# A new table of issue orders for an attention and two-mixer kernel on one core

## The chip, the cores and the metric

One core of a Trainium2 chip runs the kernel. Five engines of that core work at once: TensorE (PE, with its weight loads shown as PEld), VectorE (DVE), ScalarE (ACT), GpSimd (POOL) and SyncE (SP, which only issues DMAs). Each takes its instructions strictly in the order in which they stand in its own queue, and waits at one whose inputs or buffers are not ready, with everything behind it. The metric is the device time of one launch in microseconds.

## The reference

Float32 throughout. Attention for 4 batches, 12 heads, 448 tokens and head size 64, with an RMS norm on q and k; its output, laid out as 4 x 448 x 768, goes through two mixers.

```
q_n, k_n = rmsnorm(q, g_q), rmsnorm(k, g_k)
attn = softmax(q_n @ k_n.T / sqrt(64)) ; x = attn @ v
u = x + (x.T @ U @ V).T                    # mixer a, rank 32 over the tokens
x = u + relu(u @ w_ch1) @ w_ch2            # 768 -> 3072 -> 768
u = x + (relu(x.T @ w_tok1) @ w_tok2).T    # mixer b, 448 -> 256 -> 448
x = u + relu(u @ w_ch1) @ w_ch2            # 768 -> 1536 -> 768
```

## The kernel before

Every float32 operand of a product is kept as two rounded parts (hi and lo), and a product is three matmuls: hi by hi, lo by hi, hi by lo. So between two products an ACT instruction writes the hi part and a DVE or POOL instruction the rest. The channel weights come in as 64-bit words: `to_f32` (lines 123 to 141) rounds them on ACT (L132, L137), DVE (L133, L134, L138: tile `w_bits`) and POOL (L141), and `split` (L151 on ACT, L152 on POOL) makes the two parts.

The order of the work: attention of batches 0 and 1 alone (to about 180 us). Then mixer a on batches 0 and 1 while the attention of batches 2 and 3 runs beside it (to about 600 us), mixer b on batches 0 and 1 (to about 980 us), and then mixers a and b on batches 2 and 3, taken as a pair (`pair_ffn`) by a scheme that saves matmuls at the price of more additions on DVE and POOL.

Names that the text uses:

- `load_pair` squares q and k (L380, tile `sq`), sums (L381, `ms`), forms the scale (L383 to L391, `nt`, `rs`) and scales (L399, `qn`, `kn`). `turn_pair` transposes them on PE (L420, `tt`), and ACT and DVE write the parts (L427, L428, L431, L432, tile `both`), which DMAs place as `qs` and `ks`.
- `softmax` multiplies (`sc`), takes the maximum on DVE (L461, `nm`), the exponential on ACT (L463, `p`), and scales on POOL (L470). `weigh` transposes the probabilities on PE, four 112 x 112 blocks to a bank (L489, `pt`), splits them (L500, L504) and multiplies by v (`pv`).
- In the mixers `first` makes `ps_g`, and `relu` its parts (L657 on ACT, L658 on DVE, tile `gs`); `second` makes `ps_x`, which DVE adds to `xT` (L688), and so frees the bank. In `pair_ffn` the products are `ps_p` (first layer) and `ps_x` (second layer). DVE adds from PSUM in L781 and L853, ACT copies from PSUM in L803; `parted` (L786 on ACT, L787 on DVE) makes parts of sums that lie in SBUF; L799 is a difference, on POOL or on DVE; and `join` (L864 to L880) adds up large pieces at the end of each pair, on POOL (L864, L867, L868, L878) and DVE (L870, L873, L876, L880).

Which buffers are used, which instructions exist and what they compute is fixed by the code. The order on each engine is set at the end: `set_order` decodes the string `ORDER`, a list of displacements for each engine, and ties each instruction to the one that is to stand before it. It acts on the five queues alike, with the DMA issues on SP among them. Nothing else depends on `ORDER`.

Of the kernel before, what the change touches and what calls it, by code (L numbers as in the profile page):

```python
# [1166 lines left out]
def set_order(tc):  # L1167
# [172 lines left out]
```

## Time and profile before

| | |
|---|---|
| median of 3 runs | 1509.82 us (1508.5 to 1512.07) |
| the profiled execution | 1512.63 us |
| its span, first to last instruction | 1510.9 us |
| PE busy | 1435.4 us (95%), 7396 matmuls |
| DVE busy | 1193.6 us (79%) |
| POOL busy | 906.7 us (60%) |
| ACT busy | 737.5 us (49%) |
| mean granted TensorE clock | 0.99 |

An instruction's own time on DVE and POOL includes what it waits after it was started, so a row that is long for its kind shows such a wait inside the instruction, and not as idle time. Idle time stands in square brackets behind a row, with what ended it.

### The profile page before, as it was taken

How to read it: one execution, taken by the hardware profiler on the slowest of the kernel's cores; microseconds unless marked ns; L12 is line 12 of the kernel's file. 1: busy time of each engine (PE TensorE's matmuls, PEld its weight loads, DVE VectorE, ACT ScalarE, POOL GpSimd, SP SyncE). 2: the span in 40 equal slices, each digit the busy share in tenths (PEclk: the TensorE clock that was granted, in tenths of full speed). 3: DMA queues.
4: the chain of work that ended last, by engine and by line, in shares of the span. 5: the costliest groups of instructions: out<-in, count | busy, mean ns of one | idle time of the engine just before them, and what ended most of it. 6: DMA issues, size and time to landing. Idle time of an engine off the chain costs nothing.

```text
span 1510.9 us, 21970 instructions
## 1 busy us (share of the span) xinstructions
PE 1435.4 (95%) x7396; PEld 1262.2 (84%) x7396; DVE 1193.6 (79%) x1805; ACT 737.5 (49%) x1508; POOL 906.7 (60%) x943
## 2 busy tenths in 40 slices
PE   5999888999999999999999999999999998999998
PEld 3766666889888889888899998889889987999987
DVE  7998878887887887766867865777888888668886
ACT  4887755666656666334544443344433331335431
POOL 5999846787776665445664643067768864206760
PEclk9999989999999999999999999999999999999999
DMA  6775655776857765765457765445353453334343
GB/s 171 186 183 130 156 174 160 244 237 192 254 165 240 236 188 191 242 208 185 159 197 248 260 203 180 158 154 170 122 169 124 147 182 115 97 108 164 116 125 103
DMA packets 144384, 266.05 MB, mean 176 GB/s; under 512 B 12832, under 2 KB 104448, under 8 KB 144160
## 3 DMA queue, kind: packets, MB, share of 16 engines
q1 hardware_dynamic: 143952, 264.65, 56.5%
q8 instruction: 59, 0.97, 0.3%
q14 instruction: 53, 0.43, 0.1%
q10 hardware_dynamic: 320, 0.00, 0.0%
HBM read 149.72 MB, written 79.10 MB: 151 GB/s over the span
## 4 chain that ended last, share of the span: by engine, by line
PE 69%; DVE 13%; POOL 5%; DMA 5%; issue 3%; ACT 3%; SPq 1%; ACTq 0%; POOLq 0%; DVEq 0%
PE ps_x L81 26%; PE ps_g L81 16%; PE ps_p L81 9%; PE pv L81 4%; PE sc L81 4%; PE pt L489 3%; PE ps_u L81 2%; DVE gs L787 2%; PE ps_t L81 2%; DMA ks<-both 2%; DVE xT L853 1%; POOL p L470 1%; PE pt_x L572 1%; DVE pu L799 1%; DVE w_bits L133 1%
## 5 line engine op out<-in xcount | busy, mean ns | idle before, releaser
L81 PE MATMUL ps_x<-gs,w 128*128 128x448 f32 x1440 | 331.5, 371 | 9.2 <-DVE xT L688 8.7
L81 PE MATMUL ps_g<-u,w 128*128 128x448 f32 x1440 | 329.5, 372 | 3.8 <-DVE gs L658 2.6
L81 PEld LDWEIGHTS ps_x<-gs,w 128*128 128x128 f32 x1440 | 266.4, 189 | 36.3 <-DVE xT L688 13.3
L81 PEld LDWEIGHTS ps_g<-u,w 128*128 128x128 f32 x1440 | 268.8, 189 | 28.5 <-DVE gs L658 3.4
L81 PE MATMUL ps_x<-gs,w_b 128*128 128x448 f32 x1026 | 236.1, 372 | 14.4 <-DVE xT L853 7.2
L81 PEld LDWEIGHTS ps_x<-gs,w_b 128*128 128x128 f32 x1026 | 192.7, 190 | 36.9 <-DVE gs L787 6.9
L141 POOL TENSOR_TENSOR w_bits<-w_bits,w_round 128x768 uint32<-128x768 uint32 (+3 forms) x80 | 142.0, 1775 | 116.4 <-DVE w_bits L138 48.8
L152 POOL TENSOR_TENSOR w<-w_bits,w 128x768 fp32r<-128x768 f32 (+3 forms) x82 | 148.1, 1811 | 91.1 <-ACT w L151 71.2
L152 POOL TENSOR_TENSOR w_b<-w_f,w_b 128x384 fp32r<-128x384 f32 x104 | 120.9, 1183 | 97.1 <-ACT w_b L151 94.9
L688 DVE TENSOR_TENSOR xT<-ps_x,xT 128x448 f32<-128x448 f32 x216 | 131.4, 619 | 51.0 <-PE ps_x L81 49.1
L470 POOL TENSOR_SCALAR p<-p,sm 112x448 f32<-112x448 f32 x192 | 130.1, 687 | 35.9 <-DVE sm L467 30.4
L463 ACT ACTIVATE p<-sc,nm 112x448 f32<-112x448 f32 x192 | 120.9, 634 | 48.3 <-DVE nm L461 44.9
L461 DVE TENSOR_REDUCE nm<-sc 112x1 f32<-112x448 f32 x192 | 114.0, 616 | 18.1 <-PE sc L81 17.6
L81 PE MATMUL sc<-ks,qs 128*112 128x448 f32 x384 | 120.2, 404 | 6.4 <-ACT p L463 4.5
L489 PE MATMUL pt<-ident,p 112*112 112x112 f32 x768 | 110.5, 261 | 4.7 <-POOL p L470 3.8
L500 ACT ACTIVATE ph<-pt 112x448 fp32r<-112x448 f32 (+1 forms) x168 | 87.7, 543 | 54.6 <-PE pt L489 46.0
L489 PEld LDWEIGHTS pt<-ident,p 112*112 112x112 f32 x768 | 85.9, 133 | 29.6 <-issue 7.3
L787 DVE TENSOR_TENSOR gs<-pu,gs 128x448 fp32r<-128x448 f32 x98 | 97.1, 1009 | 9.3 <-ACT gs L786 9.2
L302 POOL TENSOR_TENSOR w_f<-w_f 128x384 f32<-128x384 f32 x26 | 28.9, 1112 | 124.8 <-DMA w_f<-c_a 83.6
L81 PE MATMUL ps_p<-t,w_b 128*128 128x448 f32 x432 | 97.0, 367 | 1.4 <-ACT pu L803 1.0
L132 ACT ACTIVATE w_bits<-w_raw 128x768 f32<-128x768 f32 (+3 forms) x80 | 69.7, 873 | 52.3 <-POOL w L152 26.1
L504 DVE TENSOR_TENSOR pl<-pt,ph 112x448 fp32r<-112x448 f32 x144 | 86.1, 616 | 11.1 <-ACT ph L500 10.4
(141 smaller groups left out, 2681.6 us busy)
## 6 DMA issues: line engine op xcount, KB each, us to landing
w_raw<-in_moe_w_ch_dram SPq DMA_DIRECT2D x72, 768.0 KB, 5.1
w_b<-h_a SPq DMA_DIRECT2D x65, 384.0 KB, 4.4
h_a<-w SPq DMA_DIRECT2D x56, 384.0 KB, 4.4
ks<-both SPq DMA_DIRECT2D x92, 224.0 KB, 4.2
c_a<-w_bits SPq DMA_DIRECT2D x40, 384.0 KB, 3.7
w_f<-c_a SPq DMA_DIRECT2D x40, 384.0 KB, 4.5
h_b<-w SPq DMA_DIRECT2D x32, 384.0 KB, 3.4
w_b<-h_b SPq DMA_DIRECT2D x29, 384.0 KB, 4.3
```

Of the source, the lines that this page charges most:

```text
L81: nc.tensor.matmul(o, lhsT=l, rhs=r, start=start, stop=stop)
L132: nc.scalar.activation(f(w), f(high), AF.Abs)
L141: nc.gpsimd.tensor_tensor(w, w, r, op=ALU.add)
L152: nc.gpsimd.tensor_sub(lo, w, f(hi))
L461: nc.vector.tensor_reduce(nm, sc, axis=AX.X, op=ALU.max, negate=True)
L463: nc.scalar.activation(p, sc, AF.Exp, bias=nm, accum_out=sm[:, c % 2:c % 2 + 1])
L470: nc.gpsimd.tensor_scalar(x, x, sm[:, i:i + 1], 1.0, op0=ALU.mult, op1=ALU.mult)
L489: nc.tensor.transpose(pt[:, c * CP:(c + 1) * CP], pr[c][:, kc * CP:(kc + 1) * CP], ident[:CP, :CP],)
L500: nc.scalar.activation(ph, pt, AF.Copy)
L504: nc.vector.tensor_sub(pl, pt, f(ph))
L688: nc.vector.tensor_add(xT[:, dc], px, xT[:, dc])
L787: nc.vector.tensor_sub(s[:, 1], t, f(s[:, 0]))
```

## The change

Only the string `ORDER` is replaced: 121 lines of it by 131. The same instructions with the same operands and buffers stand on each engine in another order. Most of them move by a few places: counted over the whole program, an instruction on PE moves by 5.6 places on the mean (82 at most), on DVE, ACT and POOL by 2.1, on SP by 2.6.

```diff
 ORDER = (
-    'c-rk<33B8(uDwtyLR>{f-~V2pz<VG;Ntt%Js;6gubeNE<(kY1x2x7<n+LxckpDn)*{%q}`r8-;xZg2fkX4_v|buCIu{RiJ'
...
+    'c-rlKiIUv9j_ePWBE(&a^Z)<#h|B~@sZ{N5+h^{~yon;zc9leN0YGd7_t$>=G<~-Gs`_llYwKT}_y-Da4gIslSK4RkPg&_'
...
 )
```

First place: DVE in mixer b of batches 0 and 1, about 631 to 640 us into the run. `w_bits_8019` and `w_bits_8221` are two blocks of raw weights in work, `gs_7842` and `gs_7864` the lo parts behind two first-layer products. Before:

```order
L138 SCALAR_TENSOR_TENSOR w_bits_8019<-w_raw_8017,w_bits_8019 128x768
L133 TENSOR_SCALAR w_bits_8221<-w_bits_8221 128x768
L134 TENSOR_SCALAR w_bits_8221<-w_bits_8221 128x768
L138 SCALAR_TENSOR_TENSOR w_bits_8221<-w_raw_8219,w_bits_8221 128x768
L658 SCALAR_TENSOR_TENSOR gs_7842<-ps_g_7823,gs_7842 128x448
L658 SCALAR_TENSOR_TENSOR gs_7864<-ps_g_7845,gs_7864 128x448
```

The same engine and place now:

```order
L138 SCALAR_TENSOR_TENSOR w_bits_8019<-w_raw_8017,w_bits_8019 128x768
L658 SCALAR_TENSOR_TENSOR gs_7842<-ps_g_7823,gs_7842 128x448
L133 TENSOR_SCALAR w_bits_8221<-w_bits_8221 128x768
L134 TENSOR_SCALAR w_bits_8221<-w_bits_8221 128x768
L138 SCALAR_TENSOR_TENSOR w_bits_8221<-w_raw_8219,w_bits_8221 128x768
L658 SCALAR_TENSOR_TENSOR gs_7864<-ps_g_7845,gs_7864 128x448
```

The first L658 stands ahead of the three steps on the second weight block. On ACT its partner L657 has likewise moved, from behind L132 and L137 of that block to ahead of them.

Second place: DVE and POOL where mixer a of batches 2 and 3 ends, about 1249 to 1272 us. `gs_139xx` are parts that the last second-layer products read, `xT_9365` and `xT_11068` the two batches' results, `w_b_13981` the parts of a weight block. DVE before:

```order
L787 TENSOR_TENSOR gs_13926<-pu_13924,gs_13926 128x448
L799 TENSOR_TENSOR pu_13931<-pu_13852,pu_13924 128x448
L853 TENSOR_TENSOR xT_11068<-ps_x_14006,xT_11068 128x1344
L853 TENSOR_TENSOR xT_11068<-ps_x_14019,xT_11068 128x1344
L787 TENSOR_TENSOR gs_13933<-pu_13931,gs_13933 128x448
L799 TENSOR_TENSOR pu_13939<-pu_13885,pu_13931 128x448
L787 TENSOR_TENSOR gs_13936<-pu_13929,gs_13936 128x448
L787 TENSOR_TENSOR gs_13941<-pu_13939,gs_13941 128x448
L658 SCALAR_TENSOR_TENSOR gs_14003<-ps_g_13984,gs_14003 128x448
```

DVE now:

```order
L853 TENSOR_TENSOR xT_11068<-ps_x_14006,xT_11068 128x1344
L799 TENSOR_TENSOR pu_13931<-pu_13852,pu_13924 128x448
L799 TENSOR_TENSOR pu_13939<-pu_13885,pu_13931 128x448
L787 TENSOR_TENSOR gs_13933<-pu_13931,gs_13933 128x448
L787 TENSOR_TENSOR gs_13926<-pu_13924,gs_13926 128x448
L787 TENSOR_TENSOR gs_13941<-pu_13939,gs_13941 128x448
L787 TENSOR_TENSOR gs_13936<-pu_13929,gs_13936 128x448
L658 SCALAR_TENSOR_TENSOR gs_14003<-ps_g_13984,gs_14003 128x448
L853 TENSOR_TENSOR X_11705<-ps_x_14034,X_11705 128x1344
L853 TENSOR_TENSOR xT_11068<-ps_x_14019,xT_11068 128x1344
L870 TENSOR_TENSOR X_11705<-X_11705,X_11704 128x1344
```

POOL before:

```order
L152 TENSOR_TENSOR w_b_13966<-w_f_13823,w_b_13966 128x384
L864 TENSOR_TENSOR xT_9365<-xT_9365,X_11704 128x1344
L152 TENSOR_TENSOR w_b_13981<-w_f_13823,w_b_13981 128x384
L867 TENSOR_TENSOR xT_11068<-xT_11068 128x1344
L868 TENSOR_TENSOR xT_11068<-xT_11068,x22_13964 128x1344
L878 TENSOR_TENSOR xT_11068<-xT_11068,X_11705 128x1344
```

POOL now:

```order
L799 TENSOR_TENSOR pu_13929<-pu_13852,pu_13921 128x448
L152 TENSOR_TENSOR w_b_13981<-w_f_13823,w_b_13981 128x384
L864 TENSOR_TENSOR xT_9365<-xT_9365,X_11704 128x1344
L867 TENSOR_TENSOR xT_11068<-xT_11068 128x1344
L878 TENSOR_TENSOR xT_11068<-xT_11068,X_11705 128x1344
L868 TENSOR_TENSOR xT_11068<-xT_11068,x22_13964 128x1344
```

On DVE the two L799 and the four L787 now stand together, ahead of the second L853 on `xT_11068`, for which L867 waits. On POOL the large L864 now stands behind the L152 on `w_b_13981`, whose ACT partner L151 has moved behind the four L786 and one L657.

Third place: PE beside attention, about 242 to 252 us, where the transposes of probabilities (`pt`) stand between the matmuls of a first layer (`ps_g`). Before:

```order
L420 MATMUL tt<-ident,kn 128x112 x4
L489 MATMUL pt<-ident,p 112x112 x3
L81 MATMUL ps_g<-u,w 128x448 x5
L489 MATMUL pt<-ident,p 112x112
L81 MATMUL ps_g<-u,w 128x448 x13
L81 MATMUL sc<-ks,qs 112x448 x4
L489 MATMUL pt<-ident,p 112x112 x4
L81 MATMUL ps_g<-u,w 128x448 x18
```

The same two banks of `pt` now:

```order
L81 MATMUL ps_g<-u,w 128x448 x3
L489 MATMUL pt<-ident,p 112x112
L81 MATMUL ps_g<-u,w 128x448 x4
L489 MATMUL pt<-ident,p 112x112
L81 MATMUL ps_g<-u,w 128x448
L489 MATMUL pt<-ident,p 112x112
L81 MATMUL ps_g<-u,w 128x448
L489 MATMUL pt<-ident,p 112x112
L81 MATMUL sc<-ks,qs 112x448 x4
L81 MATMUL ps_g<-u,w 128x448 x3
L489 MATMUL pt<-ident,p 112x112
L81 MATMUL ps_g<-u,w 128x448
```

The transposes, which stood in runs of three or four, stand singly between matmuls. Over the whole program the runs of transposes (L489, L420, L572, L1016) go from 316 to 660, those of one transpose from 60 to 474; and a transpose of L489 or L420 that is followed at once by a matmul with 128 weight columns is there 383 times, against 168.

## Rows read from the trace of the kernel before

**Rows 1.** The page: the span, and each engine's busy time.

```profile
span 1510.9 us, 21970 instructions
PE 1435.4 (95%) x7396; PEld 1262.2 (84%) x7396; DVE 1193.6 (79%) x1805; ACT 737.5 (49%) x1508; POOL 906.7 (60%) x943
```

**Rows 2.** Windows (stretch, length, busy us of PE, PEld, DVE, ACT, POOL, clock, DMA).

```profile
8.00:26.00 18.00, 8.87 (x30) 6.07 (x30) 15.35 (x27) 6.56 (x18) 9.41 (x17) 1.00 0.70 169
334.00:340.00 6.00, 4.09 (x23) 3.42 (x22) 2.40 (x5) 3.33 (x8) 4.42 (x5) 1.00 1.04 342
636.00:646.00 10.00, 8.07 (x33) 7.01 (x32) 5.69 (x6) 3.96 (x7) 3.69 (x2) 0.83 0.94 314
1006.00:1022.00 16.00, 13.60 (x63) 11.29 (x62) 12.12 (x13) 7.93 (x17) 13.63 (x13) 1.00 0.41 131
1113.00:1131.00 18.00, 16.45 (x82) 14.96 (x81) 17.54 (x17) 7.58 (x16) 11.66 (x10) 1.00 0.50 164
1204.00:1212.00 8.00, 6.66 (x33) 5.76 (x32) 7.37 (x8) 2.09 (x4) 7.77 (x8) 1.00 0.56 170
1245.00:1276.00 31.00, 23.71 (x106) 20.28 (x106) 28.76 (x22) 4.01 (x8) 18.76 (x9) 0.94 0.53 158
1454.00:1483.00 29.00, 26.55 (x128) 23.28 (x127) 26.41 (x22) 6.07 (x12) 18.91 (x9) 1.00 0.35 101
```

**Rows 3.** Windows at the lower clock: after the first place's stall, then the second's.

```profile
641.10:644.40 3.30, 3.30 (x10) 2.94 (x9) 0.29 (x1) 0.00 (x0) 0.00 (x0) 0.50 0.80 256
1272.60:1279.30 6.70, 5.98 (x16) 5.33 (x17) 1.29 (x2) 0.00 (x0) 0.00 (x0) 0.50 0.14 58
```

**Rows 4.** Timeline of the start: start, length, instruction, count, idle time and its releaser.

```profile
13.26 0.53 ACT L431 ACTIVATE both<-tt 128x448 fp32r<-128x448 f32 x1
...
15.89 0.61 DVE L432 TENSOR_TENSOR both<-tt,both 128x448 fp32r<-128x448 f32 x1
...
16.50 1.00 PE L420 MATMUL tt<-ident,qn 112*128 112x112 f32 x4 [3.94 <-DVE both L432]
```

**Rows 5.** Timeline at the first place.

```profile
635.83 0.56 DVE L134 TENSOR_SCALAR w_bits<-w_bits 128x768 uint32<-128x768 uint32 x1
...
639.58 5.67 PE L81 MATMUL ps_g<-u,w 128*128 128x448 f32 x19 [1.93 <-DVE gs L658]
```

**Rows 6.** Timeline at the second place.

```profile
1256.62 0.61 DVE L787 TENSOR_TENSOR gs<-pu,gs 128x448 fp32r<-128x448 f32 x1
...
1260.26 3.30 POOL L868 TENSOR_TENSOR xT<-xT,x 128x1344 f32<-128x1344 f32 x1
1260.59 3.99 DVE L787 TENSOR_TENSOR gs<-pu,gs 128x448 fp32r<-128x448 f32 x2
...
1264.09 1.70 PE L81 MATMUL ps_x<-gs,w_b 128*128 128x448 f32 x7 [2.89 <-DVE gs L787]
```

**Rows 7.** Timeline at 255 us: a DVE instruction beside POOL, and PE's next stall.

```profile
255.17 4.29 DVE L134 TENSOR_SCALAR w_bits<-w_bits 128x768 uint32<-128x768 uint32 x1
...
257.24 1.81 POOL L152 TENSOR_TENSOR w<-w_bits,w 128x768 fp32r<-128x768 f32 x1
...
260.65 1.68 PE L81 MATMUL ps_x<-gs,w 128*128 128x448 f32 x7 [2.88 <-DVE xT L688]
```

**Rows 8.** Chain of waits: a long run of matmuls alone (start, length, count).

```profile
859.47 14.59 PE ps_g L81 x72
```

**Rows 9.** Timeline of PE: transposes in a group.

```profile
253.21 0.93 PE L489 MATMUL pt<-ident,p 112*112 112x112 f32 x8
253.98 0.55 PE L420 MATMUL tt<-ident,qn 112*128 112x112 f32 x4
```

**Rows 10.** Timeline of PE: one transpose, two matmuls, one transpose.

```profile
512.72 0.26 PE L489 MATMUL pt<-ident,p 112*112 112x112 f32 x1
512.75 0.65 PE L81 MATMUL ps_g<-u,w 128*128 128x448 f32 x2
513.24 0.26 PE L489 MATMUL pt<-ident,p 112*112 112x112 f32 x1
```

More of the change, by code (lines that the diff above doesn't have):

```diff
@@ new lines @@
+    'EEg?TD|w$~Oj=#3yG`gVY{L3-9S}_7t$*layg)B4%wm-`z4q4WrIMr>81x=T<5v3U-x|JTFIx(j)a*R#Hr&gw+WgxGtwGJ'
+    '2^WNbj&9VvQQJ+n#7|0Eb*E)pbd;KE{`UA%|XA!Kb-_!BfQ2C*ooqdk-k@OlV!P=g0?;PAIa#_jXqtVg+OBO@WBf;3@?i|'
+    '+M73vk!mdVUZnU$_H7V_l*l7t2agz3M`aa-$uWwpyYl&|!6VZ0NJ{%V*dVc_Bo5kdX)Tc?fc%!ftnqOW$xEcRG6mIfw&8Q'
+    'xQHS-n^G5Ccguj=IAG&()%3@PraXJ+SNWI@&BZq+DTP1S?WvFjwxqAhOrAlneVHyB;GZqS%V?XbyD_vuq2UO?l=r=F4<mr'
+    'ubNhf<0Oq+ZRX{Uxo|Y))`JFGA7LnKfa_m(Qv`ObnQ}Zh>>pimqFX*)t_d$aNgre7Z+xs^&M>RBub*ESESxXyXzwP#UX7-'
@@ new lines @@
+    '=1f@djtkB5qwk&1bFvqNKc@7E6}`R{U;x|4`OEQRxnPps*%$k@j0Nj$74t9RwP2`#fJJa<{qp6>@7ZsxUZB}NmXFobrpVr'
+    'BwJskBU&%zl2-wmA2*xox*nbVBSNzT{^`uFBy`jBGTE0!Jt!hzsti@Z~JKWdETNzjeWIZY39T#bar9PFCOzJ8TyuNfE*{_'
+    'Dq{kubDv+q`E+GwltYeNpBy`4ZB+f}yK*L4%py3}%5*;?o0jo;UAmF>uo{I{b(7(Xh>&G?(G?+e7eTp&>`xvr?>pncE`9m'
+    'pE1E?E%vXg_~Zwh{ncM~SGfqK}&iNGlvWA=q69Uize-C9f$MWm;Dn`fa3R-A1p|>8ch9=IA(NBHc-?Ye&z{fL_0q-o$*tn'
+    'f}G$0}!qlw*??78RVtc;<xPb>BuTdKp%1GcoawrT3D!_WeBi_Sddz{ig&4x%bUHgEW^{#<7S+&nc&`%$kLkJ@z3zQ?qGod'
@@ new lines @@
+    'G9XsrWp#?<gDI#G)!L3<8#L{$kz*b<=8=F|bh*8c@2x=TZGh_%LBRXo$nH(V7L8Ia-4Dt2Uze@VVg;#g36i8SF`JM?(Kl('
+    'ykQm&@ZUy6Coe-@6t7-rQ8}S9^idG|mYNhlI5afagD@b)PY-k+lkkaJB&1QH9oU}3oK<FIJ1~dZa<CN<%xN%zalog<!b>!'
+    'F$IVixL9Ff7MAuByWbCHwM^CWz-sLUTam+AvzSQU*$ns%Zl8)#iKY+u00VClkFU^Hp{b1917MiaM<*eY}(8*1EmVlbl_R{'
+    'H;=eRt~>7p(qdEXxQii<Z#hco88EiS{Vg6{AiF?FRsa*-<m@Mx?F(HNv+4+r1|s?)zl?--Yl!Xb)zG)PQ2O5~WYfQ>C_M2'
+    '%RMs_NLb~sI743OcvB4YS1gG_1m*$aGq9dwl1npN9aC0EH)8_OU96G<w<df8>!#dnK)K2iVZ2UAIWCSSSHB4_gjjqVO$4^'
@@ new lines @@
+    '^7$RmWeP4sD>B0n8L0#QQ0%qE+kQN(;h_XTj+5BG0g%~~aRck1y^VTMUsM{tt)%--?>1eXI&HaX;GHc!!+ja=JjO6>0msT'
+    '<8oWWrLIAnrz5}*1K11EV4Sl&CCA2>F*~)jG3>}~PLX*yPfz8nDc<*H`SmI3vYry4$GujT5z_xY*43B%IHuwkB*RfC?anS'
+    '9bLWm9r05Wa@P)ZG^`UeP9n<0|T>=QhU$~o&gZ5##0WFO$%hwNmFa*G3wXZ#6$j0_AX9om6+G;2^XIl`u(fm3vJY#EDFE8'
+    '|V5DuUyfkP(2jKZRmMX!hw$0QI&XK{O`PnSS>5Hs%blF*kW@C2NSBrD9r)uuX<E%EnYlHUd`e2UmLItJSE6gT?RjBbYE8_'
+    'WsOX0H;Y6S<qiq4+4JP$8UzZD-5!f6nq{)VjCXA-qS>m2qGXaihyJUdvG*OxP^dwsMa%3#5HWNs-RwV6g6V7`i!+2#u+kN'
@@ new lines @@
+    '9pFZXzPI}mU_+B3HW!I0)-OZv^Wab#s}D4b?TeheUiSR63x*YT7ET}a#)2s^@jUkL047Mn##jFe^Z^}ZXe7Uah4fYkR;L7'
+    'DhtQ&A=n24&PJzK@*Pxm4Fu&b5@81EY#{^r%Y`K18<w0N=Q!ik%zCwU{VfUG(wFpi?$o4zDO~vQ;<At(^+2BsjJ8%gs4dR'
+    'F`yCz~8w|RhQlA-7!n(QdPZtbvf4t<3%uz9yt0b^zW{16z6IgHOGj*tD{uo?f49DiGBtS*zijnV!9g0Y2abR7hJtP&xVgZ'
+    'l7tG13rV=t1YDP?eb%BW6gWz<Y{*HX!kSBk$JQ1LZS7&`nZJ&6E)&iGtnP#pF=P!p5gy1EF$};NCh{b(G3?e1l+PD1Z(g&'
+    'ixI!zk*~$ZEARzjRXE4H6aOv5<oDNBet`R?=W&ryalsq+!h!749SMSCtd=C-3vE~ZDMdAj#d{-Mr56Rv|D-{?U*LRr8UGy'
@@ new lines @@
+    'JLD4(O&f_sRQ}r-6a?`7dlxzzo-Yv!BaHXQa)~=$aNaNBgjqCyzJ&7_W*^<HI>VV+Nyfb<t^+Ax1A$d8$pn*Wt2Y_fp2dh'
+    '5A|ANYrW$t_UINA+mdne<#6W}17)7k8qz_?*OKax^RLZ4vSO73HCkSz)BmuLp(UIMki1wsaOj_e5N^*cj=Hn%z*|xC2=m^'
+    ')5Um}LWEICQ0s+fYHk7$kr&}8*N17Ux>q&mqK1P|_cx$yTWIKZJfW-x`0+s>+=a^NKbiL##T3pn7wXjNW}DMS!M)*vR>Av'
+    '#_snt?l`z-vn2CDE6@ULq*4D@+lyRWdITGgVAShfl0>5x^y4-pk2Lta+H(bcr=+KI%#=#0Rs603R@7elc8%){6cFz+@$0z'
+    '=d?4E)k-R5iuO9$s|g#Iv5&+`O$w*{(D|7(X=}=rh?V<HIJx-Rq(6Jb#4zZkd4CEPcJbDj;Q%HQz{GvrXL>0{>+4#HD|s?'
@@ new lines @@
+    'td~+TkDN<PM{%k&s<1)Elz`A`0_7U_BnPb~lE(|o(c=(yDoxe?nswGpH$`wk`hJ%I5gE8cU-$1^64}W*QVB8%>>z$|X)>B'
+    'xZD0mr*u)P4m~2O|1TJ5R+_)rqnCrJM2~=rXV<4DU#K6oP`w9M@um*upKnx!*SPA`tr4<5?UDCc|@imCX`OgD)B<n`u@0+'
+    'c*5n{Z_VWxbLW&hxkFv@XYj;*qQBM#vBf&F~AB;%-!<{*rO0T{FMloXpdlno+%?c<w+7x63c7V;}%tS$+B(W_*=3`{D1DP'
+    'HqFYOW_nQPnWO15*$$Qvg=>gG)Si0VcXFmx!ngn(f{$5o;{CV82kt0m*9g(Yk2L`xQSHOzHd~8AmtBS)?u8?4yvt;*RGF9'
+    '>ywyM&ja&_S3~)0046{9p!pS;P57!j|*qslvZ$|vuMK4stG@v7UKHF#pZuNe*$1m*qx9ZjQYU6&xL-TE+)jrlR~Vht$n^='
@@ new lines @@
+    'Sr()|Hwlw;{OYmKG-4QD8v*R((8c~YKzD2u*)Nv_4dWye;7DU7w~-bq=#~at*i2+hx$#?=vh9*G+{ghxZKh=aA7K9e*2T='
+    'rd;WY&qC@D53+B(f2@clcX!BezBzn1|Gkm6r3nf>dbPS~NC8xR62&@paho5jaNCbKXW|>o6|I#HHQv!D~u8aA%wqPMLn<^'
+    'NZ(I@71Hoz|_pBI|_a7o$MrYHspW?)MlDEbFW-5+0!{2j#7+Xs3F)91pt|J}>KSMz`L694C2KG?<nI<yb)U3<}AX@^^OfA'
+    'CDH{|8^e4;-2QKf?as@WYr^h4LxJ(t<6%^DHCN@5STQhI{l6VMIJAVjO!Rx)k!u@*Yo3ICr@COg9x=;#C))<iRja#nWNKh'
+    '6jf(4#y>UgW(LiJ*c9t64B8=%DdOGK0~43?Se>ZTNgG;_7KyE7`cGRxZR@S?AL-Ql1kSjLI6zJGV7TMFxGOf{^rkAz>q0G'
```

210 lines of the change are left out of this document (90 added, 120 removed).

## The prediction

> **What bounds the kernel now.** The page comes first: PE is busy for 1435.4 us of a span of 1510.9 [rows 1], so it bounds the kernel. Since both kernels run the same instructions, an order can win only PE's idle 75.5 us and what half clock costs, and lose only what new waits add. Next come the windows of the stretches in which PE stood longest and the order around the stall has changed [rows 2]: length less PE's busy time is 9.13 us at the start, 1.91 at 334, 1.93 at 636, 2.40 at 1006, 1.55 and 1.34 at 1113 and 1204, 7.29 at 1245 and 2.45 at 1454; together 28.0 in 136 us. The other 47.5 us lie in the other 1374.9 us, 3.5%, in many short waits. I count 3.5% of each window as of that kind and not to be won. The timelines then name the instruction that ends each stall, and the windows at the lower clock show what follows two of them: after both PE runs at a granted clock of 0.5, the lower level, 1.2 GHz [rows 3].
>
> Two facts about DVE carry much of what follows. An L134 takes 0.56 us alone [rows 5] and 4.29 beside POOL instructions, an L152 of 1.81 among them [rows 7]. An L787 takes 0.61 alone, and two of them 3.99 with a POOL L868 of 3.30 beside them [rows 6]. So a small DVE instruction that reads only SBUF stands until POOL is through, and where it stands in the order decides what it meets.
>
> **The change, part by part.** What is won:
>
> Start. PE waits 3.94 us for L432 on `kn` [rows 4]. Its input, ACT's L431, is written at 13.79 (13.26 + 0.53), but L432 starts only at 15.89, behind four instructions on the next pair's squares. Now it stands four places up, ahead of them, and on POOL the next pair's scale stands ahead of two parts of `v`. That is 15.89 − 13.79 = 2.1 us won. Bounds: 0, if the DMA that places `ks` becomes the last to come, and 3.9. The squares come later by one L432, 0.61; the scale that uses them comes earlier, since the two `v` parts no longer stand ahead of it on POOL, and covers that.
>
> At 334. PE stands before a `sc` that needs a bank; in the new order that matmul comes 31 places later and `ps_g` matmuls stand in its place. 1.91 − 0.21 = 1.7 won; bounds 0 and 1.9.
>
> At 636, the first place of the order. PE's 1.93 us end with an L658 [rows 5] that stands behind three steps on a weight block; now they stand behind it, on ACT too. Idle 1.93 − 0.35 = 1.6. After it PE ran at the lower clock: ten matmuls took 3.30 us [rows 3], where long runs give 14.59/72 = 0.203 each [rows 8], 2.03 for ten: 1.3 lost. Sum 2.9; bounds 0 and 3.2. Behind the L658 that may now wait stand the three steps and then POOL's part of the block. No stall read here ends with a weight block, which is the cover. If it is gone, PE loses one L658 of delay per block, about 0.6.
>
> At 1006. One stall ends with an L803, another with an L853. They move up five places and three. 2.40 − 0.55 = 1.9; bounds 0 and 2.4.
>
> At 1113 and 1204. An L853 ends each stall; it moves up five and six places, past L781, L787 and the like. 2.89 − 0.90 = 2.0; bounds 0 and 2.9.
>
> At 1245, the second place. Idle 7.29 − 1.07 = 6.2. Half clock after it: 16 matmuls were busy for 5.98 us [rows 3], 3.25 at 0.203, so 2.7 lost. I leave one block standing: in the new order an L787 or the L870 still meets one of the large POOL instructions L864, L867 and L868. Its price is 3.99 − 0.61 = 3.4 [rows 6]. 6.2 + 2.7 − 3.4 = 5.6; bounds 2.2 with two blocks and 8.9 with none.
>
> At 1454. The same seam for the second pair. The L787 on which PE waits moves only one place and POOL's L864 still stands beside L799. I take half of 2.45 − 1.00, 0.7; bounds 0 and 1.5.
>
> Together 2.1 + 1.7 + 2.9 + 1.9 + 2.0 + 5.6 + 0.7 = 16.9 us.
>
> What is lost: first the transposes, the third place. Eight in a group take 253.98 − 253.21 = 0.77 us, 0.096 each [rows 9]. From one to the next with two matmuls between are 0.52 us [rows 10]; less two times 0.203 a single one costs 0.115. The 0.019 more I charge to those followed by a matmul with 128 weight columns, as in that row: 383 − 168 = 215 more, 4.0 us. Bounds: 0, and 6.4 if each of the 660 − 316 = 344 further runs pays it.
>
> Second, the many places that are not named here. The order moves there too, mostly by two to six places; some waits get longer, others shorter. At 255 the L688 on which PE waits 2.88 us keeps its place [rows 7] and I expect that stall to stay, neither won nor lost. For the rest the trace of before has nothing that bounds it but such stalls: I take one of 2.9 us as lost, net, with bounds of two lost (−5.8) and two won (+5.8).
>
> 16.9 − 4.0 − 2.9 = 10.0 us. The profiled execution took 1512.63, 1.73 more than its span, and that edge stays: 1502.6. The median of the three runs is 1509.82, 2.81 below the profiled one, so as a median 1499.8.
>
> A rule of the Trainium skill bears on the second place. By the page "SBUF — State Buffer", section "Who interferes with whom", DVE and GpSimd share one pair of ports as an exclusive lock: whoever issues first keeps it for its whole instruction, and the other stands still. The L787 beside one L868 agrees. The L134 with 4.29 − 0.56 = 3.7 us of wait, more than the L152's 1.81 [rows 7], stood past one instruction, which the rule as written does not give. By the rule the block left at the second place is 3.4 at most; by the L134 it could be 6.8, and the sum 6.6 instead of 10.0.
>
> **The rivals.** All goes. Every named stall is won but its 3.5%, 28.0 − 4.7 = 23.3, and both half clocks, 4.0; nothing else is lost but the transposes: 27.3 − 4.0 = 23.3, so 1486.5. For it: in each of these places the instruction PE waits on has moved ahead of something. Against it: 9.13 us of this are the start, where loads and a chain of small instructions come one after the other, and at 1245 DVE is busy 28.76 of 31 us, so the additions themselves fill the stretch.
>
> The waits only move. What DVE waits behind POOL depends on which of the two starts first, in either order of the program. Where L799 and four L787 move ahead of one large POOL instruction, they come nearer to the one before, and an L853 behind them is late instead. If new waits cost 12.9 us instead of 2.9, four or five places like the one at 255, the sum is nought and the time 1509.8. For it: DVE is busy 79% and POOL 60% [rows 1], so most moved instructions meet another. Against it: in the first two places the gain does not hang on what POOL does alone, since steps of three weight operations or four squares are passed.
>
> Slower: the transposes hold their banks. Four in a group fill a bank of `pt` in 0.39 us. In the new order a bank is filled by singles with six matmuls between, 4 × 0.115 + 6 × 0.203 = 1.7 us, so it stays taken 1.3 us longer before ACT and DVE can empty it. Beside mixer a run the attention's 2 × 12 heads with four banks each, 96 banks. If PE waits w per bank for the next to come free, the loss is 96 w. At w = 0.13 the 12.9 us that remain of 16.9 after the 4.0 are gone, and from there it is slower; at 0.3, about a quarter of the 1.3, it is 28.8 + 4.0 − 16.9 = 15.9 us, 1525.7. For it: spread transposes also delay the probabilities' parts. Against it: PE has other matmuls between them, and the stall that the rows show of this stage ends with an L688 [rows 7], not with a bank of `pt`.
>
> **How the numbers follow.** The forecast gets 0.55, with its own range 1491 to 1506: ten us gained, give or take the second place's other bounds (−3.4, +3.4) and one or two stalls elsewhere. All goes: 0.09. Waits only move: 0.22, centred on 1509.8 and 3 to 4 us to either side. Slower by the banks: 0.14. Two tenths of a percent, about what a measurement of this kernel can tell, are 3.0 us, 1506.8 to 1512.8. Faster: 0.55 + 0.09 + 0.07 of the third = 0.71. Same: 0.11 of the third and 0.01 of the banks = 0.12. Slower: 0.04 of the third and 0.13 of the banks = 0.17. The range reaches from 1483, under the case that all goes, to 1513; what lies above is most of the last rival and a little of the one before, and below hardly anything.
>
> **What would show it.** Right: the stall that ended at 16.50 ends some 2 us earlier; no stretch at clock 0.5 after 640 and after 1270, with idle under 0.5 us around 636 and under 4 around the second place; there one DVE instruction of 3 to 4 us and not two; PE busy 1431 to 1437 us (the transposes add 4, the clock gives 4 back), so the gain lies in idle time, about 65 us of it. Wrong: DVE instructions of over 3 us at other places with PE waiting behind them (waits that moved); idle time of PE in front of `pt` matmuls in many small pieces between 180 and 600 (banks); a new stretch at the lower clock, which costs 1.3 to 2.7 us each.

## The result, and the profile after

| | before | changed |
|---|---|---|
| median (4 runs each) | 1510.31 us | 1469.21 us (1468.44 to 1470.06) |
| span of the profiled execution | 1510.9 us | 1466.7 us |
| PE idle (span less busy) | 75.5 us | 46.5 us |
| DVE busy | 1193.6 us | 1133.0 us |

The ratio is 0.9728, with an interval of 0.9711 to 0.9745: 41 us, or 2.7%, less. The forecast was 1500 with a range of 1483 to 1513. The direction was right; the gain is four times what the sum gave, and lies outside the range. The page of the changed kernel, to be read against [rows 1]:

```profile
span 1466.7 us, 21966 instructions
PE 1420.2 (97%) x7396; PEld 1252.8 (85%) x7396; DVE 1133.0 (77%) x1805; ACT 735.6 (50%) x1508; POOL 899.3 (61%) x943
```

DVE does the same 1805 instructions in 60.6 us less. Which ones, the groups by line show (busy, mean ns, idle before). The kernel before:

```profile
L688 DVE TENSOR_TENSOR xT<-ps_x,xT 128x448 f32<-128x448 f32 x216 | 131.4, 619 | 51.0 <-PE ps_x L81 49.1
L787 DVE TENSOR_TENSOR gs<-pu,gs 128x448 fp32r<-128x448 f32 x98 | 97.1, 1009 | 9.3 <-ACT gs L786 9.2
L138 DVE SCALAR_TENSOR_TENSOR w_bits<-w_raw,w_bits 128x768 uint32<-128x768 uint32 (+3 forms) x80 | 93.0, 1162 | 1.6
L133 DVE TENSOR_SCALAR w_bits<-w_bits 128x768 f32<-128x768 f32 (+3 forms) x80 | 71.4, 892 | 18.5 <-ACT w_bits L132 18.2
L134 DVE TENSOR_SCALAR w_bits<-w_bits 128x768 uint32<-128x768 uint32 (+3 forms) x80 | 65.5, 818 | 1.8
L799 DVE TENSOR_TENSOR pu<-pu 128x448 f32<-128x448 f32 x28 | 38.2, 1366 | 2.6 <-POOL pu L799 2.4
```

The changed kernel:

```profile
L688 DVE TENSOR_TENSOR xT<-ps_x,xT 128x448 f32<-128x448 f32 x216 | 131.6, 618 | 59.8 <-PE ps_x L81 56.5 <-PE pt_x L572 2.0
L787 DVE TENSOR_TENSOR gs<-pu,gs 128x448 fp32r<-128x448 f32 x98 | 80.9, 850 | 7.1 <-ACT gs L786 7.1
L138 DVE SCALAR_TENSOR_TENSOR w_bits<-w_raw,w_bits 128x768 uint32<-128x768 uint32 (+3 forms) x80 | 78.7, 984 | 1.8
L133 DVE TENSOR_SCALAR w_bits<-w_bits 128x768 f32<-128x768 f32 (+3 forms) x80 | 55.7, 696 | 10.6 <-ACT w_bits L132 10.4
L134 DVE TENSOR_SCALAR w_bits<-w_bits 128x768 uint32<-128x768 uint32 (+3 forms) x80 | 55.4, 693 | 1.9
L799 DVE TENSOR_TENSOR pu<-pu 128x448 f32<-128x448 f32 x28 | 28.2, 1006 | 3.6 <-POOL pu L799 3.4
```

The five lines whose inputs lie in SBUF lose 66 us between them. L688, which takes one input from PSUM, takes 619 and 618 ns. So nothing became quicker in itself: DVE stood less inside its instructions, and the runs with POOL's work cut, below, show that a large part of this standing is a wait for POOL. It has not all gone (an L787 alone takes 610 ns, the mean is still 850), but PE now waits 0.3 us for L787 where it waited 4.9. Nor was it handed to POOL on the whole: POOL's busy time fell too, from 906.7 to 899.3 us.

The windows of the changed kernel (stretch, length, busy us of PE, PEld, DVE, ACT, POOL, clock, DMA) that answer to [rows 2] follow. Each runs between the same places in PE's sequence of matmuls as its window of before, to 0.1 us. The last alone does not: it starts at 270 us in both kernels and holds 37 matmuls fewer in the changed one.

```profile
160.00:267.80 107.80, 93.76 (x483) 76.42 (x482) 93.22 (x161) 67.85 (x147) 71.57 (x86) 0.94 0.63 189
325.10:329.30 4.20, 4.20 (x24) 3.78 (x22) 3.79 (x8) 1.35 (x2) 4.20 (x4) 1.00 0.43 151
620.80:627.10 6.30, 6.30 (x32) 5.83 (x32) 3.74 (x5) 2.24 (x5) 3.88 (x3) 1.00 0.44 144
982.90:996.40 13.50, 13.14 (x63) 11.35 (x63) 10.19 (x11) 7.05 (x15) 10.76 (x10) 1.00 0.55 168
1086.60:1103.00 16.40, 16.40 (x81) 14.86 (x80) 14.72 (x16) 7.02 (x16) 14.36 (x13) 1.00 0.30 93
1175.40:1181.70 6.30, 6.30 (x33) 5.76 (x32) 5.56 (x7) 3.93 (x8) 5.51 (x6) 1.00 0.66 178
1213.90:1236.20 22.30, 21.76 (x107) 19.66 (x107) 18.38 (x20) 4.18 (x8) 17.10 (x9) 1.00 0.52 169
1412.80:1438.90 26.10, 26.10 (x128) 23.69 (x128) 21.66 (x24) 6.10 (x13) 19.33 (x10) 1.00 0.28 78
270.00:1455.00 1185.00, 1181.86 (x6111) 1069.05 (x6111) 894.34 (x1349) 547.63 (x1040) 692.29 (x599) 1.00 0.56 183
```

and two windows of before that no row of the prediction shows:

```profile
160.20:275.10 114.90, 96.67 (x481) 76.82 (x481) 93.22 (x160) 67.37 (x146) 71.78 (x86) 0.93 0.58 169
270.00:1499.00 1229.00, 1199.57 (x6148) 1084.20 (x6147) 959.08 (x1359) 554.71 (x1049) 704.89 (x605) 1.00 0.56 178
```

The last line of each is the finding: from 270 us to near the end PE stood 29.4 us before and 3.1 after (the same, if both are taken from the matmul at 275 us of before). In five of the seven windows behind 270 us it does not stand at all. The first place of the order now has no stretch at the lower clock, nor has the second. What each stretch won, from the starts of the same matmuls in both kernels, against the terms:

| stretch of before | predicted to be won | measured |
|---|---|---|
| start to 160 us | 2.1 | 0.2 |
| 160 to 275 | 0 | 7.1 |
| 334 | 1.7 | 1.8 |
| 636 | 2.9 | 3.7 |
| 1006 | 1.9 | 2.4 |
| 1113 and 1204 | 2.0 | 3.3 |
| 1245 to 1276 | 5.6 | 8.8 |
| 1454 | 0.7 | 2.6 |
| everywhere else | −2.9 | 14.3 |
| transposes | −4.0 | (inside the stretches above; see Transposes below) |

"Everywhere else" is the 44.2 us between the spans less the other stretches; it lies in 5.9 us from 275 to 604, 4.5 up to 1004 and 3.9 behind.

How the second place looks now, in the timeline of the changed kernel (start, length):

```profile
1219.66 1.28 DVE L799 TENSOR_TENSOR pu<-pu 128x448 f32<-128x448 f32 x2
1220.93 2.23 DVE L787 TENSOR_TENSOR gs<-pu,gs 128x448 fp32r<-128x448 f32 x4
...
1224.00 3.09 POOL L864 TENSOR_TENSOR xT<-xT,X 128x1344 f32<-128x1344 f32 x1
1225.29 3.88 PE L81 MATMUL ps_g<-u,w_b 128*128 128x448 f32 x18
...
1226.96 1.55 DVE L870 TENSOR_TENSOR X<-X 128x1344 f32<-128x1344 f32 x1
1227.12 4.33 POOL L867 TENSOR_TENSOR xT<-xT 128x1344 f32<-128x1344 f32 x1
...
1234.60 3.09 POOL L868 TENSOR_TENSOR xT<-xT,x 128x1344 f32<-128x1344 f32 x1
1234.65 3.52 DVE L873 TENSOR_TENSOR X<-X,X 128x448 f32<-128x448 f32 x1
```

Against [rows 6]: the two L799 and four L787 run through in 3.5 us, because POOL's L864 has not begun; two L787 alone took 3.99 before. Where DVE's L870 meets POOL, it is POOL's L867 that was started later, and it is L867 that is long (4.33 us, 3.40 before). PE does not wait for it. The page "SBUF — State Buffer" of the Trainium skill, section "Who interferes with whom", says that issue order decides who blocks; this pair agrees with it. One meeting went the other way: L873 stands 3.52 us beside L868, which started 0.05 us ahead of it. PE's only stall behind it is 0.37 us, on an L888.

### The profile page after: what moved, and what is told of

The parts are those of the page before. It is cut to its first block, busy times and chain, and to the rows that moved or that the text cites. A ratio compares the mean times of both kernels' runs of the same rounds, so it can differ in the third digit from the quotient of the medians.

```text
span 1466.7 us, 21966 instructions
## 1 busy us (share of the span) xinstructions
PE 1420.2 (97%) x7396; PEld 1252.8 (85%) x7396; DVE 1133.0 (77%) x1805; ACT 735.6 (50%) x1508; POOL 899.3 (61%) x943
## 4 chain that ended last, share of the span: by engine, by line
PE 81%; DVE 7%; POOL 5%; DMA 3%; issue 2%; ACT 1%; SPq 0%; ACTq 0%; POOLq 0%; DVEq 0%
PE ps_x L81 32%; PE ps_g L81 21%; PE ps_p L81 11%; PE pv L81 3%; PE sc L81 3%; PE pt L489 3%; PE ps_u L81 3%; PE ps_t L81 2%; POOL p L470 2%; PE pt_x L572 1%; POOL sq L380 1%; PE ps_h L81 1%; DVE nm L461 1%; PE tt L420 1%; DMA qs<-both 1%
## 5 line engine op out<-in xcount | busy, mean ns | idle before, releaser
L81 PE MATMUL ps_x<-gs,w 128*128 128x448 f32 x1440 | 335.4, 375 | 5.2 <-DVE xT L688 4.7
L81 PE MATMUL ps_g<-u,w 128*128 128x448 f32 x1440 | 338.5, 378 | 0.0
L81 PEld LDWEIGHTS ps_g<-u,w 128*128 128x128 f32 x1440 | 263.0, 189 | 29.1 <-POOL w L152 0.2
L141 POOL TENSOR_TENSOR w_bits<-w_bits,w_round 128x768 uint32<-128x768 uint32 (+3 forms) x80 | 142.6, 1783 | 146.0 <-DVE w_bits L138 87.2
L152 POOL TENSOR_TENSOR w_b<-w_f,w_b 128x384 fp32r<-128x384 f32 x104 | 118.9, 1163 | 114.3 <-ACT w_b L151 114.2
L688 DVE TENSOR_TENSOR xT<-ps_x,xT 128x448 f32<-128x448 f32 x216 | 131.6, 618 | 59.8 <-PE ps_x L81 56.5
L152 POOL TENSOR_TENSOR w<-w_bits,w 128x768 fp32r<-128x768 f32 (+3 forms) x82 | 144.0, 1765 | 41.3 <-ACT w L151 38.8
L470 POOL TENSOR_SCALAR p<-p,sm 112x448 f32<-112x448 f32 x192 | 131.4, 693 | 33.8 <-DVE sm L467 28.3
L489 PE MATMUL pt<-ident,p 112*112 112x112 f32 x768 | 143.7, 260 | 5.6 <-POOL p L470 4.0
L463 ACT ACTIVATE p<-sc,nm 112x448 f32<-112x448 f32 x192 | 121.0, 634 | 38.7 <-DVE nm L461 35.6
L81 PE MATMUL sc<-ks,qs 128*112 128x448 f32 x384 | 126.7, 418 | 8.8 <-DMA ks<-both 5.4
L489 PEld LDWEIGHTS pt<-ident,p 112*112 112x112 f32 x768 | 92.5, 133 | 26.5 <-POOL p L470 8.8
L657 ACT ACTIVATE gs<-ps_g 128x448 fp32r<-128x448 f32 x88 | 47.0, 542 | 113.9 <-PE ps_g L81 113.7
L658 DVE SCALAR_TENSOR_TENSOR gs<-ps_g,gs 128x448 fp32r<-128x448 f32 x88 | 53.8, 620 | 63.5 <-ACT gs L657 63.4
L853 DVE TENSOR_TENSOR xT<-ps_x,xT 128x1344 f32<-128x1344 f32 x54 | 83.6, 1550 | 12.0 <-PE ps_x L81 11.6
```

The source lines that it names most:

```text
L81: nc.tensor.matmul(o, lhsT=l, rhs=r, start=start, stop=stop)
L141: nc.gpsimd.tensor_tensor(w, w, r, op=ALU.add)
L152: nc.gpsimd.tensor_sub(lo, w, f(hi))
L463: nc.scalar.activation(p, sc, AF.Exp, bias=nm, accum_out=sm[:, c % 2:c % 2 + 1])
L470: nc.gpsimd.tensor_scalar(x, x, sm[:, i:i + 1], 1.0, op0=ALU.mult, op1=ALU.mult)
L489: nc.tensor.transpose(pt[:, c * CP:(c + 1) * CP], pr[c][:, kc * CP:(kc + 1) * CP], ident[:CP, :CP],)
```

## The experiments

Each run's ratio is to runs of the kernel before on the same chip; microseconds are the ratio on 1510.31.

**Which engine's order: two runs.** In the first, DVE, ACT and POOL have the new order and PE and SP the old one; in the second, PE alone has the new. Where the two orders can't stand beside each other at all, the old one stays for all: 2585 of 3055 moved instructions have their new place in the first run, 4469 of 5494 in the second.

```diff
-set_order: old table on PE, DVE, ACT, POOL, SP
+run 1:     old PE, new DVE, new ACT, new POOL, old SP   (2585 instructions in another place)
+run 2:     new PE, old DVE, old ACT, old POOL, old SP   (4469 instructions in another place)
```

> The kernel before with the new order on DVE, ACT and POOL in the stretches where that can stand beside the old order on PE and SP (85 of 100 of the instructions that change place on these three engines; PE and SP as before). Theory A (the gain is where DVE and POOL instructions stand to each other, so that those on which PE waits are no longer held up): 25 to 35 us less than before, DVE busy about 1140 us. Rival B (the gain is PE's own order, which puts other ready matmuls in front of each wait): within 5 us of before, PE's idle time after 270 us still over 25 us. If neither order is worth anything without the other: no gain, or slower, with DVE busy lower all the same.

> The reverse: the kernel before with the new order on PE alone, where that can stand beside the old order of the others (4469 of 5494 moved places). Theory A: at most 10 us less than before, DVE busy still about 1190 us. Rival B: 25 to 35 us less. If the two orders only work together: slower than before.

Measured: 1642.81 us (ratio 1.0849, 1.0817 to 1.0880) and 1679.17 (1.1081, 1.1041 to 1.1120). Neither theory; the third outcome of both texts. The page of the first run, and PE's longest waits in the first and in the second (total us, times, longest), say how:

```profile
PE 1478.5 (90%) x7396; PEld 1280.6 (78%) x7396; DVE 1149.0 (70%) x1805; ACT 735.7 (45%) x1508; POOL 889.2 (54%) x943
```

```profile
PE sc L81 <- ACT p L463: 21.6, 24, 2.1
PE ps_x L81 <- DVE gs L787: 16.0, 10, 4.2
```

```profile
PE ps_x L81 <- DVE xT L688: 18.1, 22, 2.1
```

In the first run DVE is down to 1149.0 us, most of the way to 1133, and the kernel is 128 us slower. So a smaller DVE total does not make a kernel faster by itself; whether it is down by its order or because a longer run leaves more room is not shown. PE now waits 21.6 us for L463 and 16.0 for L787, which were 4.5 and 4.9 before: instructions stand on DVE, ACT and POOL in an order that no longer answers to PE's. The two halves of the table belong together, and these runs can't say which engine's order wins.

**How much is POOL's: two runs.** The orders stay whole, and POOL's work is cut; L141, L470 and the large additions do 16 columns, so their results are not computed in full.

```diff
-        nc.gpsimd.tensor_tensor(w, w, r, op=ALU.add)
+        nc.gpsimd.tensor_tensor(w[:, :16], w[:, :16], r[:, :16], op=ALU.add)
-                    nc.gpsimd.tensor_scalar(x, x, sm[:, i:i + 1], 1.0, op0=ALU.mult, op1=ALU.mult)
+                    nc.gpsimd.tensor_scalar(x[:, :16], x[:, :16], sm[:, i:i + 1], 1.0, op0=ALU.mult, op1=ALU.mult)
-            nc.gpsimd.tensor_add(c11, c11, x1)
+            nc.gpsimd.tensor_add(c11[:, 0, :16], c11[:, 0, :16], x1[:, 0, :16])
...
```

> The kernel before, its order unchanged, with POOL's in-place work cut to 16 columns: L141, L470 and the four large additions L864, L867, L868, L878 (these results are then not computed in full). L152, the sums of weights and the squares stay. Theory A (DVE's instructions on SBUF wait for POOL): L133, L134, L138, L787 fall to 0.55 to 0.75 us on the mean from 0.89, 0.82, 1.16 and 1.01, DVE busy falls by 40 us or more, PE's idle time after 270 us falls from 29 to 15 us or less, and the time to 1480 to 1495 us. If DVE is slow for another reason (its own inputs, the order alone): DVE busy stays within 10 us of 1193 and the time above 1500.

> The changed kernel with the same cut on POOL. Theory A: little of what is left of PE's time hangs on POOL's holds, so 3 to 12 us less than the changed kernel (the end of the waits for p and the start), and the two kernels come to stand less than half as far apart as 41 us. Rival: the two keep their distance of about 40 us, since the order wins by something that has nothing to do with POOL.

Measured: 1485.91 us for before with the cut (ratio 0.9817, 0.9791 to 0.9843) and 1458.34 for the changed kernel with it (0.9643, 0.9611 to 0.9675). The page line and the stretch behind 270 us of before with the cut:

```profile
PE 1430.5 (96%) x7396; PEld 1264.0 (85%) x7396; DVE 1148.9 (77%) x1805; ACT 735.9 (50%) x1508; POOL 690.2 (46%) x943
```

```profile
270.00:1474.00 1204.00, 1191.06 (x6141) 1080.69 (x6140) 914.76 (x1359) 551.78 (x1046) 536.04 (x605) 1.00 0.56 182
```

With the order untouched, DVE falls by 44.7 us and PE's idle time behind 270 us from 29.4 to 12.9. So these waits of DVE, and through them most of what PE won here, came from POOL's instructions; that part of theory A stands. (The cut also brings POOL's own results sooner: 1.6 us of PE's idle time behind 270 us were waits for L470's `p`, and they are gone.) Two of its numbers fell: L138 only came to 1.13 us and L787 to 0.94. L152 on the weights, 269 us of POOL's time in before, is uncut; that it is what they still wait for is likely and not shown. The changed kernel gains 13 us by the cut, where the text gave 3 to 12; the interval holds both. And the two kernels stay 26 us apart with it (0.9643 against 0.9817), nearly two thirds of 41: neither under half, as theory A had it, nor about 40, as the rival had it. So some 15 us of the gain go with the instructions that were cut. The other 26 I can't split further into waits on L152 and waits of another kind, as no run cuts L152.

**Single stretches: three runs.** The kernel before with the new order of all five engines in one stretch only.

```diff
-set_order: old table throughout
+run 5:     old table; 1230 to 1290 us as in the new table
+run 6:     old table; 630 to 662 us as in the new table
+run 7:     old table; 160 to 275 us as in the new table
```

> The kernel before with the new order of all five engines only in the stretch from 1230 to 1290 us (255 moved places, 176 of them on PE). By the term of the prediction 5.6 us less, with one L787 or L870 still held by POOL in front of PE; by the comparison of the two traces 8.9 us less in this stretch (PE idle 7.1 to 0.9 us, and no half clock after it). Rival: the seam was quick in the changed kernel because what stands ahead of it came differently, and alone it wins less than 3 us.

> The kernel before with the new order only from 630 to 662 us. By the term of the prediction 2.9 us less (1.6 idle, 1.3 half clock); by the comparison of the traces up to 3.9, the stall at 655 (1.2 idle) with it. Rival: nothing within 1 us, since the L658 that moved up then waits for its matmuls and the weight steps behind it come late.

> The kernel before with the new order only from 160 to 275 us, which the prediction took to win nothing. By the comparison of the traces 7.8 us less (PE idle 18.2 to 14 us, half clock 17.1 to 13.6 us and the rest in short waits). Rival: the gain came from what stands before 160 and after 275, and it is within 2 us.

Measured: ratios 0.9944 (0.9926 to 0.9963), 0.9961 (0.9945 to 0.9976) and 0.9951 (0.9934 to 0.9968), so 8.5, 5.9 and 7.4 us less. In their windows, one of each run:

```profile
1246.20:1267.70 21.50, 21.50 (x107) 19.64 (x105) 17.35 (x20) 4.18 (x8) 15.98 (x9) 1.00 0.50 160
```

```profile
634.00:646.00 12.00, 12.00 (x61) 11.02 (x59) 6.66 (x11) 6.09 (x10) 6.20 (x5) 1.00 0.72 272
```

```profile
160.50:267.80 107.30, 93.52 (x480) 75.44 (x481) 92.75 (x160) 67.72 (x145) 71.23 (x86) 0.95 0.63 190
```

The second place alone takes 21.5 us instead of 31.1, without idle time and at full clock: 9.6, more than both numbers in the text; by the run times it is 8.5. The stretch at 636 wins 3.7 us at the named stall, as in the changed kernel, and 4.8 up to 690, with the stall at 655. The stretch from 160 to 275 wins 7.6, by itself, though the prediction had put it at nothing. The rivals (no gain alone, or a gain only on the ground of the other stretches) fell in all three.

**Transposes.** The changed kernel, with the four transposes of a bank moved together to the last of them, for 108 of 129 spread banks.

```diff
-PE: L489, matmuls, L489, matmuls, L489, matmuls, L489
+PE: matmuls, L489 L489 L489 L489
```

> The changed kernel with 108 of 129 spread banks of pt filled by their four transposes in one run, at the place of the last of them on PE (runs of L489 from 414 to 182, singles from 300 to 17; nothing else moves). By the term of the prediction, 0.019 us for each of the runs that go, 232 x 0.019 = 4.4 us less. Rival: spread transposes cost nothing net, because one stands where PE would otherwise wait, and the grouped ones let the banks fill later: 0 to 10 us more, with PE idle in front of sc, pt or pv.

Measured: 1468.86 us (0.9705, 0.9681 to 0.9729), beside 0.9728 for the changed kernel: not told apart. The intervals are too wide to tell 4.4 us from nothing. Between the profiles, the grouped one is 0.8 us ahead where the last of the moved transposes has run (matmul 3200), of the 4.4 expected. Its trace shows two things that nearly cancel. From matmul 40 to 2940, counted from the start of one matmul to the next, those without a stall or the lower clock take 3.2 us less than in the changed kernel, and those with a stall take 2.1 us more. So the two texts are each borne out in part: a spread transpose costs PE a little, and some stand where PE would otherwise wait. Two profiles of one order lie 1.2 us apart in this stretch, so these are rough.

**Two halves.** The new order up to 604 us, and from there on.

```diff
-set_order: old table throughout
+run 9:     new table up to 604 us, old table behind
+run 10:    old table up to 604 us, new table behind
```

> The kernel before with the new order of all engines up to 604 us and the old one behind it. If stretches add up, as the three single stretches did: the 15.1 us that the two traces are apart there. If a late stretch wins only on the ground of the early ones: the second part goes otherwise than in before, and the sum of this and the next run is off 41 us by more than 5.

> The reverse: the old order up to 604 us and the new one behind it. If stretches add up: 29.1 us less (44.2 between the spans less 15.1), with PE's idle time behind 604 us under 2 us. Otherwise, as for the first half: off the sum by more than 5 us.

Measured: 1495.19 us (0.9889, 0.9867 to 0.9911) and 1486.18 (0.9831, 0.9807 to 0.9855): 16.8 and 25.5 us less, 42.3 together against 41, within the 5 us that the text allowed. Stretches add up. The parts that were expected, 15.1 and 29.1, lie within the two intervals. Behind 600 us the second still has 2.8 us of idle time in PE (875.00 less 872.20), not under 2:

```profile
600.00:1475.00 875.00, 872.20 (x4405) 796.32 (x4403) 647.57 (x902) 344.30 (x623) 462.64 (x351) 1.00 0.52 169
```

**POOL's hold at the second place by itself.** The kernel before, order unchanged, with only L864, L867, L868 and L878 cut as above.

```diff
-            nc.gpsimd.tensor_add(c12, c12, x5)
-            nc.gpsimd.tensor_add(x5, x5, x)
+            nc.gpsimd.tensor_add(c12[:, 0, :16], c12[:, 0, :16], x5[:, 0, :16])
+            nc.gpsimd.tensor_add(x5[:, 0, :16], x5[:, 0, :16], x[:, 0, :16])
...
```

> The kernel before, its order unchanged, with POOL's four large additions L864, L867, L868, L878 at the seams of the pairs cut to 16 columns of one of three blocks (their results are then not computed in full). If the L787 and L799 at the second place stand because POOL holds what they need: two L787 in 1.2 us and no longer 3.99, the L799 0.65 and no longer 3.51, PE's stall of 2.89 us at 1264 gone, and 6 to 9 us less at the seam (1245 to 1276), with that of the stall at 1273 if the L853 comes in time. Rival: DVE is simply full there (28.76 of 31 us), the L853 comes late all the same, and the seam wins under 3 us.

Measured: 1500.91 us (0.9926, 0.9905 to 0.9947), 11.2 less. The timeline:

```profile
1255.89 0.53 POOL L867 TENSOR_TENSOR xT<-xT 128x16 f32<-128x16 f32 x1 [2.82 <-DVE xT L853]
1256.26 0.64 DVE L799 TENSOR_TENSOR pu<-pu 128x448 f32<-128x448 f32 x1
...
1256.82 1.35 DVE L787 TENSOR_TENSOR gs<-pu,gs 128x448 fp32r<-128x448 f32 x2
1257.98 2.02 PE L81 MATMUL ps_x<-gs,w_b 128*128 128x448 f32 x9
...
1267.50 5.74 PE L81 MATMUL ps_x<-gs,w_b 128*128 128x448 f32 x27 [0.68 <-DVE xT L853]
```

The same two L787 take 1.35 us in place of 3.99, PE's 2.89 us of waiting for them are gone, and the later stall on L853 is 0.68. Four POOL instructions held the whole seam (the end of a mixer, where `join` adds up); that DVE is busy for 28.76 of 31 us there was largely that hold itself. Between the traces this seam wins 8.3 us, where the new order wins 8.8. The whole run won more than that, since the second pair's seam at 1454 gains 2.5 us too.

**A version from both.** The changed kernel, with the old order from 58 to 166 us.

```diff
-set_order: new table throughout
+run 12:    new table; 58 to 166 us as in the old table
```

> The changed kernel with the old order from 58 to 166 us, the only long stretch in which it lost: 1.9 us there against before (PE idle 3.8 to 6.6 us). If stretches add up, 1.9 us less than the changed kernel, about 1467. Rival: the early lead of 1.9 us at 58 us lasted only because of that order, or the joint breaks it: the same as the changed kernel within 1 us, or slower.

Measured: 1468.33 us (0.9714, 0.9692 to 0.9737), beside 1469.21 (0.9728). The span is 1465.0 against 1466.7. What was expected is within the interval, and so is nothing: not told apart.

## Why the prediction was wrong, point by point

- **The step that failed is the second cost, "the many places that are not named here", put at 2.9 us lost.** It is 7.1 won from 160 to 275 us and 14.3 in the other places. That puts it 24.3 us off, most of the 34.2 between the 10.0 of the sum and the 44.2 between the spans. Two thoughts in it were wrong. The 47.5 us of idle time outside the windows were taken as many short waits and as not to be won. In fact 13.7 of them lie before 8 us and behind 1499, 5.0 between 26 and 160, 18.2 from 160 to 275 and 10.6 behind; and of the 33.8 us from 26 to 1499, 36 stalls of 0.3 us or more make up 30.4. With the windows, from 270 to 1499 us, 29 such stalls make up 27.8 of 29.4 us, and the changed kernel has 4. The waits of PE by releaser, which no row of the prediction shows, list them. Before, and then after, from the second entry on (total us, times, longest):

```profile
PE ps_x L81 <- DVE xT L688: 8.7, 8, 2.9
PE ps_x L81 <- DVE xT L853: 7.2, 4, 3.3
...
PE ps_x L81 <- DVE gs L787: 4.9, 4, 2.9
PE sc L81 <- ACT p L463: 4.5, 7, 1.9
...
PE pt L489 <- POOL p L470: 3.8, 7, 1.0
PE ps_g L81 <- DVE gs L658: 3.0, 3, 1.9
```

```profile
PE sc L81 <- DMA ks<-both: 5.4, 2, 5.1
PE ps_x L81 <- DVE xT L688: 4.7, 5, 2.3
PE pt L489 <- POOL p L470: 4.0, 8, 1.2
```

L853, L787 and L658 are no longer among the reasons for more than 1 us. And a loss was charged without a row: new waits were supposed because old ones went. New ones came from 58 to 160 us, where PE's idle time goes from 3.8 to 6.6 us and 1.7 us are lost; behind 275 the three stretches and the two halves show none that weigh. Of the 14.3 us, 8.3 are idle time; the rest shows as busy time, for which see the last section.

- **Left out altogether: the stretch from 160 to 275 us.** It holds the longest stretch at the lower clock, 13.7 us in before and 10.2 after, and more idle time than the second place, 18.2 us in before and 14.0 after; its order is changed. The prediction counts the clock only behind its own two places. Of the stalls here it names the one at 255 us, which did stay (2.9 us, and 2.3 after); the gain lies in others.

- **The bound "only PE's idle 75.5 us and what half clock costs" was too tight.** PE busy was to come out at 1431 to 1437 us. It is 1420.2, with the same instructions, since part of a stall shows as busy time (last section).

- **Transposes, −4.0: mis-sized.** Grouping them in the changed kernel wins about 1 us net between the profiles, and the run times show no difference. What was charged to 215 of them was read from one row, and it left out that some can fill a place where PE would have stood.

- **The second place, 5.6: right in its mechanism, and 8.8.** A block did stay, L873 with 3.52 us beside L868, but PE stood only 0.37 us behind it. Its price was also read too high: 3.99 us are two L787, so less two times 0.61 it is 2.8 and not 3.4. The order does not merely choose which small instruction meets the large one: it has most of the small ones run before POOL's large ones start, and at L870 only POOL is late.

- **636, 1006, 1113 and 1204, 334: right**, with 3.7, 2.4, 3.3 and 1.8 for 2.9, 1.9, 2.0 and 1.7. The 3.5% kept back from each as not to be won is most of the difference. 1454 gave 2.6 for 0.7, by the same fault as the second place.

- **The start, 2.1: 0.2 by 160 us.** The DMA that places `ks` did become the last to come, which the prediction named as the case for a bound of 0:

```profile
16.90 0.68 PE L81 MATMUL sc<-ks,qs 128*112 128x448 f32 x1 [5.15 <-DMA ks<-both]
```

Even so the first `sc` starts at 16.90, where it had started at 18.14, and at 58 us the lead is 1.9 us. By 160 it is spent in the new waits.

- **The rivals.** "All goes" named the mechanism that came true, and gave 1486.5, still 17 us too slow, since it too counted only the named windows, and of a stall only its idle time. "The waits only move" fell to the single stretches; only from 58 to 160 us did waits move. "The banks" fell to the result, and to PE's waits for `p` in front of `pt`, which are 3.8 us before and 4.0 after.

## What to carry to other kernels

Before a change of order is priced, list all stalls of the bounding engine by length and releaser. Here a few dozen carried the idle time, and behind 270 us the new order took nearly all of it, 29.4 to 3.1 us: it was no background. Where small DVE instructions on SBUF are long for their kind, look which POOL instruction was started first: the small ones can be run before it starts, or the wait be left to POOL if nobody waits for POOL. An order is one thing across all engines: half of a good one was 8 to 11% slower than the old one whole, while a whole stretch of it kept its worth alone.

## What the runs showed that I had not expected

PE's idle time tells only part of what a stall costs. A matmul that stands alone in the changed kernel's timeline shows 0.36 us, while the next starts 0.21 after it:

```profile
1208.83 0.36 PE L81 MATMUL ps_p<-u,w_b 128*128 128x448 f32 x1
...
1209.04 3.85 PE L81 MATMUL ps_x<-gs,w_b 128*128 128x448 f32 x18
```

So a stall behind a matmul hides up to some 0.15 us. Of the 44.2 us between the spans, 29.0 are idle time; the lower clock accounts for about 5.8 (half of the busy time in its stretches, 22.8 us before and 11.1 after). The other 9.4 show in neither. Most of them are this hidden share. From 275 us of before on, take each matmul's time from its start to the next start, above what is usual for its shape. Those with a stall behind them sum to 36.3 us before, of which 29.4 show as idle time, and to 4.6 after, of which 3.1 do. So 5.4 of the 9.4 us are hidden shares of stalls, 0.16 us for each of the 43 of before. The rest lies almost all ahead of 275 us, and there it stays open.
